# The layer norm's weights: from a multiply of the rows on GpSimd to a multiply of W1 on ScalarE

## The chip, the cores and the metric

The kernel runs on one core of one Trainium2 chip. The metric is the device time of the program in microseconds (us); the time before is the median of three runs. One further execution was taken by the hardware profiler: its trace is what the profile shows.

The engines are called as in the profile: PE is TensorE (PEld its weight loads), DVE is VectorE, ACT is ScalarE, POOL is GpSimd, SP is SyncE, from whose queue all DMAs of this kernel are issued. Each engine works through its own instructions in a fixed order and stops at one whose inputs are not there yet.

## The reference

Attention over 8 batches, 8 heads, 576 positions, head size 64, with a mask by blocks of 64 positions; then a layer norm and a two-layer perceptron with a residual.

```python
scores = scale * np.matmul(q, k.transpose(0, 1, 3, 2))
scores = np.where(block_i >= block_j, scores, -1000000000.0)
attn = np.exp(scores - max); attn = attn / (sum + 1e-09)
x = (attn @ v)  # heads side by side: 8 x 576 rows of 512

mu, var = mean(x), mean((x - mu) ** 2)
xn = (x - mu) / np.sqrt(var + 1e-06) * g_ln
ch = np.maximum(xn @ w_ch1, 0.0) @ w_ch2      # 512 -> 2048 -> 512
return x + ch
```

`g_ln` has 512 values, one for each column of `xn`, that is one for each row of `w_ch1`.

## The kernel before

All work is written as tasks, `add(engine or engines, cost, function, r=reads, w=writes, prio=...)`. A planner (`Plan.run`, L91) goes through them in a simulated time of its own, with cost estimates for each engine and for the DMAs, gives a task that may run on several engines to one of them, and so writes the order of every engine's instructions before the program is compiled. A task that is added, removed or given another engine shifts the planner's times, and with them the order of many others, also of tasks that the edit doesn't name.

**Attention.** 32 pairs of heads, one after the other on PE (`pair`, counted from 0 here). Each has scores (PE, L396), mask and row maximum (DVE, L411), exponentials with row sums (ACT, L414), transposes (PE, L423) with their evacuation into `pt` (ACT or DVE, by the helper lines L215 and L217) and the product with V (PE, L429 and L433), whose result is transposed by DVE (L506, `ot`) and stored to DRAM in `xd`. Four times two further steps treat the first block of 64 positions (L543 to L582). Beside all this the packed weights are unpacked (`decode`: ACT, DVE and POOL, L325 to L358) into `w1f` and, for W2, `wcs` in DRAM.

**Perceptron.** 36 tiles of 128 rows are treated in five rounds of 8, 8, 8, 6 and 6 tiles. For each round `norm_tiles` treats the tiles in pairs: load (`x<-xd`, L627, four or eight small DMAs for a tile), division by the softmax sums (L636, DVE or POOL), a copy for the residual (`xrow`, L640), statistics (L645), reciprocal square root (DVE L654 to L657, POOL L663 to L666), subtract and multiply (L671, DVE), the multiply by g (L674, POOL), a transpose (L676, DVE, `xnt`) and the way through DRAM (`xw`, L680; `xt`, L684) to the transposed tile `xt`. `operands` makes from these the left operands `xm` of a seven-product scheme (differences `tt` L701, high parts by L215 or L217, low parts L712). In round 0 these steps run beside the attention.

W1 and W2 are cut into 8 groups. In round 0 `stream` loads a group of W1 (`wf<-w1f`, L765; 128 partitions, 2 blocks, 512 columns in the order of W1's rows), forms sums on POOL (L773), high parts (L215 or L217) and low parts (L784, DVE or POOL) into `wa` and `wb`, and stores these to DRAM as `was` and `wbs`; in later rounds it loads them back (L758). The first three groups are made in the last pairs of the attention, the others during round 0. `products` multiplies a group with the operands (PE, L814, seven tasks of six matmuls; evacuations L822, L827, RELU L833 on ACT and low part L834 on DVE), and `second` multiplies the result `h` with W2 (PE, L874, `y`) and adds it to `ya` (DVE, L883). In the last group of a round the sums are stored (`out_t`, L886).

The high and low parts are two float32r numbers for each value, and each product is three matmuls. An `x` tile has two buffers, and so has `wf`.

The weights g lie in SBUF as `g_sb`, before as 512 values repeated in every partition (L297 to L300).

## Time and profile before

| | |
|---|---|
| median of 3 runs | 1068.18 us (1067.79 to 1070.01) |
| the profiled execution | 1069.32 us, span 1067.5 us |
| granted TensorE clock in it, mean | 0.996 |
| ACT multiplies by g | none |
| POOL multiplies by g (L674) | 36, 48.4 us busy |
| DMA | 248.91 MB, mean 233 GB/s |

In the lines of the profile "out<-in" stands for the tile or tensor that is written and those that are read. A group's line ends with its busy time, the mean duration of one in ns, the engine's idle time just before them, and what ended most of it. In the timeline a row is a run of like instructions with its start and its duration in us, and in brackets the idle time before it and its releaser.

### The profile page before, as it was taken

The numbers are of one execution on the slowest core, as the hardware profiler recorded it, in microseconds if no ns is written. First come the engines' busy times: TensorE is split into PE (matmuls) and PEld (weight loads), VectorE is DVE, ScalarE is ACT, GpSimd is POOL, SyncE is SP. The second block draws the span as 40 slices with busy tenths as digits, with TensorE's granted clock in tenths as the row PEclk, the third lists the DMA queues.
The fourth block names the chain that finished last, engine by engine and source line by source line (L and its number), as shares of the span: only waits on it lengthen the run. The fifth ranks groups of instructions, "written<-read, shape, count | busy, mean of one in ns | idle before, by whom it ended". The sixth has DMA issues, their size and how long they took to land.

```text
span 1067.5 us, 17862 instructions
## 1 busy us (share of the span) xinstructions
PE 1049.8 (98%) x6240; PEld 856.0 (80%) x6240; DVE 789.0 (74%) x1726; ACT 450.2 (42%) x1099; POOL 292.4 (27%) x442
## 2 busy tenths in 40 slices
PE   9999999999999999999999999999999999999998
PEld 6777767667678888778888888888888888889997
DVE  6878999998978889795666794676484766854554
ACT  7767979879874333242121151121132212322221
POOL 0002546534525766270212240221010221200000
PEclk9999999999999999999999999999999999999999
DMA  5447898998979888867777746777537779865541
GB/s 188 153 141 233 216 307 271 310 296 276 324 238 321 254 305 285 259 224 256 208 235 228 222 176 249 222 206 243 170 128 277 226 255 285 272 225 215 193 159 73
DMA packets 237930, 248.91 MB, mean 233 GB/s; under 512 B 159376, under 2 KB 188048, under 8 KB 227600
## 3 DMA queue, kind: packets, MB, share of 16 engines
q1 hardware_dynamic: 237840, 247.77, 71.5%
q8 instruction: 49, 0.80, 0.3%
q14 instruction: 41, 0.34, 0.1%
HBM read 182.71 MB, written 65.01 MB: 232 GB/s over the span
## 4 chain that ended last, share of the span: by engine, by line
PE 55%; DVE 5%; POOL 2%; DMA 2%; issue 1%; SPq 1%; ACT 0%; DVEq 0%; POOLq 0%
PE y L874 30%; PE p L814 25%; DVE h L834 1%; DVE ya L883 1%; SPq L627 1%; DMA wcs<-wd 1%; DMA wc<-wcs 1%; DVE t L827 0%; POOL x L674 0%; DVE xnt L676 0%; DVE xm L712 0%; DVE wb L784 0%; DVE wa L784 0%; DVE st L645 0%; DVE sgn L342 0%
## 5 line engine op out<-in xcount | busy, mean ns | idle before, releaser
L874 PE MATMUL y<-wc,h 128*128 128x512 f32 x1728 | 438.0, 392 | 2.1 <-ACT h L833 1.8
L874 PEld LDWEIGHTS y<-wc,h 128*128 128x128 f32 x1728 | 323.7, 188 | 66.4 <-DVE h L834 2.5
L883 DVE TENSOR_TENSOR ya<-y,ya 128x512 f32<-128x512 f32 x288 | 197.2, 686 | 155.1 <-PE y L874 154.4
L814 PE MATMUL p<-xm,wa 128*128 128x512 f32 (+1 forms) x960 | 222.5, 368 | 0.1
L814 PEld LDWEIGHTS p<-xm,wa 128*128 128x128 f32 x960 | 176.2, 188 | 27.3 <-DVE xm L712 0.6
L833 ACT ACTIVATE h<-t 128x512 fp32r<-128x512 f32 (+1 forms) x120 | 62.4, 581 | 275.9 <-DVE t L827 265.9
L814 PE MATMUL p<-xm,wb 128*128 128x512 f32 (+1 forms) x720 | 167.5, 368 | 1.7 <-DVE wb L784 1.5
L814 PEld LDWEIGHTS p<-xm,wb 128*128 128x128 f32 x720 | 132.5, 188 | 23.6 <-DVE wb L784 1.9
L822 ACT COPY t<-p 128x512 f32<-128x512 f32 (+1 forms) x120 | 65.3, 545 | 192.6 <-PE p L814 189.2
L827 DVE TENSOR_TENSOR t<-p,t 128x512 f32<-128x512 f32 (+1 forms) x120 | 75.8, 632 | 42.5 <-PE p L814 40.1
L396 PE MATMUL s<-raw 64*128 64x192 f32 (+4 forms) x640 | 96.5, 435 | 1.3 <-DVE nm L411 0.6
L414 ACT ACTIVATE pab<-pab,nm 128x576 f32<-128x576 f32 (+1 forms) x128 | 91.6, 724 | 8.9 <-DVE nm L411 8.7
L396 PEld LDWEIGHTS s<-raw 64*128 64x128 f32 x640 | 60.7, 186 | 37.8 <-issue 29.5
L411 DVE CUSTOM_DVE_ANT_0 pab<-s,never 128x576 f32<-128x576 f32 (+1 forms) x128 | 83.7, 683 | 3.4 <-PE s L396 3.0
L414 ACT ACTIVATE pu<-pu,nm 128x320 f32<-128x320 f32 (+1 forms) x128 | 64.5, 508 | 38.9 <-DVE nm L411 38.7
L433 PE MATMUL o<-pt,v 128*64 128x256 f32 (+1 forms) x768 | 80.3, 344 | 0.0
L333 POOL TENSOR_SCALAR mag<-mag 128x512 f32<-128x512 f32 x32 | 51.0, 1597 | 103.6 <-ACT mag L330 103.6
L433 PEld LDWEIGHTS o<-pt,v 128*64 128x64 f32 x768 | 56.9, 137 | 26.0
L834 DVE SCALAR_TENSOR_TENSOR h<-t,h 128x512 fp32r<-128x512 f32 (+1 forms) x120 | 76.9, 694 | 0.3 <-ACT h L833 0.2
L423 PE MATMUL tr<-ident,pab 128*128 128x128 f32 x512 | 67.1, 280 | 5.2 <-DVE nm L411 2.6
L215 ACT COPY pt<-tr 128x512 f32<-128x512 f32 (+1 forms) x126 | 65.0, 580 | 3.1 <-PE tr L423 2.7
L423 PEld LDWEIGHTS tr<-ident,pab 128*128 128x128 f32 x512 | 57.4, 143 | 11.0 <-DVE pt L217 3.7
(89 smaller groups left out, 982.8 us busy)
## 6 DMA issues: line engine op xcount, KB each, us to landing
wc<-wcs SPq DMA_DIRECT2D x40, 1024.0 KB, 6.8
wa<-was SPq DMA_DIRECT2D x32, 1024.0 KB, 7.6
wb<-wbs SPq DMA_DIRECT2D x32, 768.0 KB, 5.7
raw<-qk SPq DMA_DIRECT2D x32, 576.0 KB, 5.0
wr<-w SPq DMA_DIRECT2D x32, 512.0 KB, 6.7
v<-v SPq DMA_DIRECT2D x32, 320.0 KB, 5.2
x<-xd SPq DMA_DIRECT2D x144, 64.0 KB, 3.8
xrow<-x SPq DMA_DIRECT2D x36, 256.0 KB, 5.4
```

Of the source, the lines that this page charges most:

```text
L215: e.copy(out=out, in_=in_)
L396: nc.tensor.matmul(x, raw.t[HALF[h], 0, col], raw.t[HALF[h], 1, at:at + x.shape[1]], start=True, stop=True)
L411: add("DVE", dve(n) + .01, lambda: nc.vector.tensor_tensor_reduce(out=p.t[:, part(i, h)], in0=s.t[:, cols], in1=hide, scale=-0.125, scalar ...
L414: add("ACT", act(n, True) + .14, lambda: nc.scalar.activation(out=p.t[:, part(i, h)], in_=p.t[:, part(i, h)], func=AF.Exp, bias=nm.t[:, at ...
L423: nc.tensor.transpose(o.t[:, n * P:(n + 1) * P], x, ident)
L433: nc.tensor.matmul(o.t[HALF[h], at + lo:at + 256], v_sb.t[:, ck, HALF[h]], rhs(h), start=False, stop=(n == len(steps) - 1), skip_group_che ...
L814: nc.tensor.matmul(x.t[:, 0:TN], w_(l), xs[m].t[:, 0:half, o, k], start=start and k == e == 0, stop=k == 1 and e == 2, skip_group_check=True)
L822: add("ACT", act(TN), lambda: nc.scalar.copy(out=t.t[:, 0:TN], in_=x.t[:, 0:TN]), r=[r], w=[new], prio=0)
L827: add("DVE", dve(TN), lambda: nc.vector.tensor_add(t.t[:, 0:TN], x.t[:, 0:TN], t.t[:, 0:TN]), r=r, w=[new], prio=0)
L834: add("DVE", dve(TN), lambda: nc.vector.scalar_tensor_tensor(out=x.t[:, 1, 0:TN], in0=src(), scalar=0.0, in1=x.t[:, 0, 0:TN], op0=ALU.max, ...
L874: nc.tensor.matmul(yb.t, x.t[:, l, at:at + P], wc.t[:, i, o], start=i == e == 0, stop=i == 1 and e == 2)
L883: add("DVE", dve(512), lambda yb=yb, ya=ya: nc.vector.tensor_add(ya.t, yb.t, ya.t), r=[part, before_], w=[now], prio=1)
```

## The change

The load of g brings 4 values to each partition instead of 512: the host stores g as (4, 128) transposed, so that column c of `g_sb` holds the weights of rows 128c to 128c+127 of W1, one per partition. In `norm_tiles` the task of L674 is gone and the transposes read the rows as L671 leaves them. In `stream`, in round 0, one new task for each group runs four `nc.scalar.mul` in place on the loaded W1 group, each on two blocks of 128 columns (128x256 values) with one column of `g_sb` as the factor, and all that read the group now read the scaled one.

```diff
-    g_sb = odd.tile([P, DM], F32, name="g_sb")
+    g_sb = odd.tile([P, NC], F32, name="g_sb")
     gb = Buf()
-    gsrc = bass.AP(tensor=g.tensor, offset=g.offset, ap=[[0, P], [1, DM]])
-    add("SP", .45, lambda: nc.sync.dma_start(out=g_sb, in_=gsrc), w=[gb], prio=150, size=P * 2048)
+    add("SP", .45, lambda: nc.sync.dma_start(out=g_sb, in_=g), w=[gb], prio=150, size=P * 16)
...
-            unit, scaled = Buf(parent=x), Buf(parent=x)
+            unit = Buf(parent=x)
...
-            add(any_of(lambda e, x=x: e.tensor_mul(x.t, x.t, g_sb), POOL=pool(512)), r=[unit, gb], w=[scaled], prio=prio)
             xnt, xw = new_xnt(), new_xw()
-            add("DVE", dve(512), lambda x=x, xnt=xnt: nc.vector.transpose(xnt.t, x.t), r=[scaled], w=[xnt], prio=prio)
+            add("DVE", dve(512), lambda x=x, xnt=xnt: nc.vector.transpose(xnt.t, x.t), r=[unit], w=[xnt], prio=prio)
...
         fetch(2, 3)
+        raw = wf
+        wf = Buf(parent=raw)
+
+        def by_g():
+            for c in range(NC):
+                x = raw.t[:, :, P * c:P * c + P]
+                nc.scalar.mul(x, x, g_sb[:, c:c + 1])
+        add("ACT", 4 * act(256, True), by_g, r=[raw, gb], w=[wf], prio=prio)
...
-        "g": gl.reshape(1, -1).copy(),
+        "g": np.ascontiguousarray(gl.reshape(4, 128).T),
```

The planner's new order. Line numbers after the change are lower by one or two in the first part and higher by up to six behind the new task: the product is L814 before and L820 after, `y` L874 and L880, `ya` L883 and L889, the multiply by the sums L636 and L635, the mask L411 and L410.

On DVE, where the last masks of pair 13 stand, before (a row of `ISA` is a mask with its row maximum or the read of that maximum; `xm`, `st`, `norm` are those named above):

```order
L411 ISA pab,nm<-s,never 128x576
L411 ISA nm 128x1
L411 ISA pab,nm<-s,never 128x448
L411 ISA nm 128x1
L217 CAST xm_1623<-xt 128x256
L217 CAST xm_1626<-tt 128x256
L636 TENSOR_TENSOR x<-x,sums_all 128x512
L712 TENSOR_TENSOR xm_1626<-tt,xm_1626 128x256
L645 BN_STATS st<-x 128x6
L646 BN_AGGR norm<-st 128x2
```

and in the changed program:

```order
L410 ISA pab,nm<-s,never 128x576
L410 ISA nm 128x1
L635 TENSOR_TENSOR x<-x,sums_all 128x512 x2
L644 BN_STATS st<-x 128x6
L645 BN_AGGR norm<-st 128x2
L644 BN_STATS st<-x 128x6
L645 BN_AGGR norm<-st 128x2
L581 STREAM_TRANSPOSE ot_1639<-o 128x256 x2
L653 TENSOR_SCALAR norm<-norm 128x2
L655 TENSOR_SCALAR norm<-norm 128x2
L656 TENSOR_SCALAR norm<-norm 128x2
L410 ISA pab,nm<-s,never 128x448
```

Both tiles' multiplies, their statistics and the first step of the reciprocal root now stand ahead of the pair's last mask; before, they stood behind it, the second of them in the next pair.

On PE at the end of round 0, where the last group's products, its `y` and round 1's first products meet, before (the product with `xm_1540` is the first of a group's seven, the one that reads `xm_1704` the last):

```order
L874 MATMUL y<-wc,h 128x512 x24
L814 MATMUL p<-xm_1540,wa 128x512 x6
L814 MATMUL p<-xm_1559,wa 128x512 x6
L814 MATMUL p<-xm_1626,wa 128x512 x6
L874 MATMUL y<-wc,h 128x512 x18
L814 MATMUL p<-xm_1623,wa 128x512 x6
L814 MATMUL p<-xm_1688,wb 128x512 x6
L814 MATMUL p<-xm_1693,wb 128x512 x6
L874 MATMUL y<-wc,h 128x512 x6
L814 MATMUL p<-xm_1704,wb 128x512 x6
L874 MATMUL y<-wc,h 128x512 x6
L814 MATMUL p<-xm_1540,wa 128x512 x6
```

and in the changed program (here `xm_1523` marks the first of the seven and `xm_1744` the last):

```order
L820 MATMUL p<-xm_1710,wb 128x512 x6
L880 MATMUL y<-wc,h 128x512 x12
L820 MATMUL p<-xm_1525,wa 128x512 x6
L880 MATMUL y<-wc,h 128x512 x6
L820 MATMUL p<-xm_1744,wb 128x512 x6
L880 MATMUL y<-wc,h 128x512 x54
L820 MATMUL p<-xm_1523,wa 128x512 x6
L820 MATMUL p<-xm_1545,wa 128x512 x6
L820 MATMUL p<-xm_1708,wa 128x512 x6
L820 MATMUL p<-xm_1531,wb 128x512 x6
```

Before, the last `y` tasks of round 0 stand between the products of round 1; now nine of them (54 matmuls) run in one row and round 1's products follow in another.

On SP at the same place, before (`wf` is the last W1 group, `xw` and `xt` the pieces of round 1's tiles):

```order
L680 DMA xw<-xnt 32x16x32 x7
L758 DMA wc<-wcs 128x2048
L680 DMA xw<-xnt 32x16x32
L684 DMA xt<-xw 128x4x128
L627 DMA x<-xd 32x16x32 x8
L684 DMA xt<-xw 128x4x128
L792 DMA wbs<-wb 128x1536
L765 DMA wf<-w1f 128x1024
```

and in the changed program, from the load of the last W1 group on; rows between the two pieces are left out:

```order
L763 DMA wf<-w1f 128x1024
L682 DMA xt<-xw 128x4x128
L639 DMA xrow<-x 128x512
L756 DMA wc<-wcs 128x2048
L798 DMA wbs<-wb 128x1536
L678 DMA xw<-xnt 32x16x32 x8
```

```order
L678 DMA xw<-xnt 32x16x32
L682 DMA xt<-xw 128x4x128
L892 DMA out_t<-ya 128x512 x6
L682 DMA xt<-xw 128x4x128
L892 DMA out_t<-ya 128x512
```

The load of the last W1 group has moved ahead of pieces of round 1's tiles behind which it stood, and the second `xt` of round 1's last pair stands behind six stores of round 0's results. On DVE, in the changed program, the rows at the same place are these:

```order
L710 TENSOR_TENSOR xm_1744<-tt,xm_1744 128x256
L889 TENSOR_TENSOR ya<-y,ya 128x512 x8
L217 CAST xm_1523<-xt 128x256
L699 TENSOR_TENSOR tt<-xt 128x256
L710 TENSOR_TENSOR xm_1523<-xt,xm_1523 128x256
L217 CAST xm_1545<-tt 128x256
```

Eight additions to `ya` stand ahead of the last operand pieces of round 1's first product, which reads `xm_1523`.

## Prediction

> **What bounds the kernel now.** I read the page first, its busy rows and the chain that ended last, then stretches of time, then the matmuls' own timeline at the places where a stretch shows TensorE less than full.
>
> ```profile
> span 1067.5 us, 17862 instructions
> PE 1049.8 (98%) x6240; PEld 856.0 (80%) x6240; DVE 789.0 (74%) x1726; ACT 450.2 (42%) x1099; POOL 292.4 (27%) x442
> PE 55%; DVE 5%; POOL 2%; DMA 2%; issue 1%; SPq 1%; ACT 0%; DVEq 0%; POOLq 0%
> ...
> 162.74:171.53 8.79, 8.79 (x78) 6.53 (x77) 8.53 (x23) 7.65 (x22) 6.37 (x7) 1.00 0.88 227
> ...
> 171.53:181.72 10.19, 10.19 (x79) 7.09 (x77) 10.19 (x29) 10.10 (x28) 7.36 (x16) 1.00 1.00 371
> 181.72:192.23 10.51, 9.90 (x110) 7.07 (x109) 9.73 (x29) 9.78 (x29) 4.66 (x5) 1.00 0.74 180
> 192.23:201.78 9.55, 9.49 (x76) 6.64 (x77) 9.26 (x30) 8.45 (x24) 6.02 (x7) 1.00 1.01 292
> 201.78:213.33 11.55, 10.88 (x143) 8.02 (x141) 11.41 (x34) 9.74 (x29) 8.18 (x19) 1.00 1.00 347
> ...
> 250.00:270.00 20.00, 20.00 (x203) 14.64 (x199) 15.73 (x48) 20.00 (x56) 8.62 (x8) 1.00 0.80 274
> ...
> 440.00:460.00 20.00, 18.11 (x72) 14.19 (x71) 16.65 (x33) 5.66 (x11) 11.36 (x20) 0.91 0.81 297
> 460.00:480.00 20.00, 18.28 (x79) 14.49 (x79) 18.67 (x40) 9.22 (x24) 14.75 (x15) 1.00 0.71 233
> 480.00:1064.00 584.00, 583.75 (x2716) 499.96 (x2715) 373.09 (x681) 132.10 (x272) 88.78 (x180) 1.00 0.66 215
> ```
>
> A stretch's columns are its length, then busy time of PE, PEld, DVE, ACT and POOL, the clock, the DMA share and GB/s. Three things are to be seen. From 480 us on TensorE is busy 583.75 of 584.00 us: nothing that the other engines save there can shorten the run. In the attention, which ends near 317 us, DVE and ACT fill their stretches (10.19 and 10.10 of 10.19). And between 440 and 480 us TensorE lacks 1.89 and 1.72 us and has a lower clock in the first half. So the change can only be worth something in the attention and in the hand-over from round 0 to round 1. A busy TensorE in the attention isn't at its peak, since a matmul that waits may be drawn long; there I go by the time from one pair's scores to the next. The first five stretches run from the scores of one pair to those of the next: the undisturbed pair takes 8.79 us, the four behind it 10.19, 10.51, 9.55 and 11.55.
>
> **The change: removed and added work.**
>
> ```profile
> L674 POOL TENSOR_TENSOR x<-x,g_sb 128x512 f32<-128x512 f32 x36 | 48.4, 1355 | 21.9 <-DVE x L671 19.4 <-DMA wa<-was 1.4 <-DMA ya<-xrow 0.7
> L676 DVE STREAM_TRANSPOSE xnt<-x 128x512 f32<-128x512 f32 x36 | 25.3, 704 | 7.3 <-POOL x L674 7.2
> L215 ACT CAST xm<-tt 128x256 fp32r<-128x256 f32 x46 | 16.8, 408 | 10.3 <-POOL tt L701 5.1 <-PE p L814 3.8 <-POOL xm L712 1.4
> L414 ACT ACTIVATE pu<-pu,nm 128x320 f32<-128x320 f32 x64 | 36.0, 563 | 37.8 <-DVE nm L411 37.8
> L414 ACT ACTIVATE pu<-pu,nm 128x192 f32<-128x192 f32 x64 | 29.1, 454 | 1.0 <-DVE nm L411 0.9
> ```
>
> GpSimd loses 36 multiplies of 1355 ns, 48.4 us. It is 27% busy and has 2% of the chain, so this is worth only what its lateness costs: DVE stood 7.2 us before the transposes for it, about 0.2 us in each of 36. Each tile is ready 1.36 us sooner. The load of g shrinks to 2 KB per core; nobody waited for the old one.
>
> ScalarE gains 32 multiplies of 128x256 with one value per partition. The trace has none. Below it stands the cast of the same size without such a value, 408 ns; above it the exponential of 128x320 with a bias per partition, 563 ns; halfway in size between that and the 192-wide one (454) is 508. I take 0.46 us, halfway between 408 and 508: 1.84 us for a group's four, 14.7 us for the eight groups (13.1 to 18.0). [...] Five of the eight groups are made in round 0, where ACT is busy 43.86 of 112 us (the row stands further down), and TensorE's products are their cover; if that cover were gone they would cost 9.2 us. Three groups, 5.5 us, are made in the last pairs of the attention. There ACT is busy 20.00 of 20.00 us, so these are on the path unless DVE takes something over, which it does in part: DVE has 15.73 of 20.00, and the planner moves casts and evacuations of `pt`. The bounds are 0 and 5.5 us. Since TensorE is full beside ACT in that stretch, a pair takes whichever is longer, and I take +1.0, with the one product that no longer stands between the last two PV blocks in it.
>
> **Moved: pair 13's masks.** The new order runs both multiplies by the softmax sums (L636 of before) ahead of the last mask of this pair.
>
> ```profile
> 131.98 2.91 PE L396 MATMUL s<-raw 64*128 64x320 f32 x20
> ...
> 136.65 0.66 PE L423 MATMUL tr<-ident,pu 128*128 128x128 f32 x4 [1.17 <-DVE norm L654]
> 137.88 3.66 PE L423 MATMUL tr<-ident,pab 128*128 128x128 f32 x16 [0.57 <-DVE nm L411]
> ...
> 144.65 1.56 PE L396 MATMUL s<-raw 64*128 64x320 f32 x10
> ...
> 310.29 1.91 PE L423 MATMUL tr<-ident,pab 128*128 128x128 f32 x16
> ...
> 134.14 0.69 DVE L636 TENSOR_TENSOR x<-x,sums_all 128x512 f32<-128x512 f32 x1 [2.33 <-DMA x<-xd]
> ...
> 135.09 0.69 DVE L645 BATCH_NORM_STATS2 st<-x 128x6 f32<-128x512 f32 x1
> ...
> 130.67 0.76 DVE L582 STREAM_TRANSPOSE ot<-o 128x256 f32<-128x256 f32 x2
> ...
> 127.41 0.61 DVE L411 CUSTOM_DVE_ANT_0 pab<-s,never 128x448 f32<-128x448 f32 x1
> ...
> DMA to landing us min/median/max: 2.0/3.9/10.9
> ```
>
> The last row is the landing of the pieces of x (L627). Pairs are counted from 0; 131.98 is the start of pair 14. Before, DVE stood 2.33 us for the second tile until 134.14, behind that came the masks of pair 14, and the pair took 12.67 us (131.98 to 144.65) instead of 8.79: 3.9 us lost, of which 1.75 by sixteen transposes that ran in 3.66 us after the idle (1.91 in the last pair, at 310.29). In the changed program the same wait stands one pair sooner. Behind it in DVE's order come the second tile's multiply and statistics (0.69 and 0.69), two `ot` transposes (0.76), some 0.6 us of small steps and the mask that frees the score banks (0.61): 3.4 us from the landing to that mask's end. Before, this mask was done at 128.0, 4 us ahead of pair 14's scores, so there is that much room. If the eight pieces land at 131 to 132, since they follow each other on SP without gaps now, the scores start at 134.4 to 135.4 and a clean pair then brings pair 15 to 143.2 to 144.2 instead of 144.65; with the slow transposes again that is +0.3 to +1.3. Bounds: a landing at 129 or sooner gives 3.4 back, one at 135.5 loses 5.0 (rival 2). I take +0.5.
>
> **Moved: the third and fourth norm, 171.53 to 213.33.** These four stretches lose 10.19+10.51+9.55+11.55-4x8.79 = 6.6 us against clean pairs. Some 2 us of that is a first block's own work on TensorE, which stays: three steps of 32 small matmuls, 0.69 us each by the row below.
>
> ```profile
> 171.00:215.00 44.00, 0.69 (x32) 0.56 (x32) 1.00 0.94 300
> ```
>
> That leaves 4.6 us, and DVE is full or nearly so in all four (10.19 of 10.19 to 11.41 of 11.55), so an instruction taken off it there counts. The third norm's tiles come sooner by the 1.36 us of the missing multiply and the new order brings their transposes ahead into pairs where DVE had room; the pair with the softmax of a first block and the one behind it hand one multiply (0.69 us above), the reciprocal of the sums and five `pt` evacuations to their neighbours, which are full in part themselves. Bounds: 0, and -4.6. I take -1.0 for the first of these stretches (it lost 1.4) and -2.2 for the other three (3.2).
>
> **Moved: round 0 to round 1.**
>
> ```profile
> 447.25 0.63 ACT L215 CAST wa<-wf 128x512 fp32r<-128x512 f32 x1 [11.55 <-DMA wcs<-wd]
> ...
> L765 SPq DMA_DIRECT2D wf<-w1f x8: 326/430/659, 255.4 to 440.5; - x8
> ...
> 450.49 6.33 PE L874 MATMUL y<-wc,h 128*128 128x512 f32 x18 [1.81 <-ACT h L833]
> 456.66 4.24 PE L814 MATMUL p<-xm,wa 128*128 128x512 f32 x18
> ...
> 468.30 2.56 PE L814 MATMUL p<-xm,wb 128*128 128x512 f32 x10 [1.51 <-DVE wb L784]
> ...
> 472.43 1.66 PE L814 MATMUL p<-xm,wb 128*128 128x512 f32 x6 [0.21 <-DVE t L827]
> ```
>
> The last W1 group's load was issued at 440.5, behind tile pieces on SP's queue, and landed with ACT already waiting in front of its cast; the RELUs behind that cast came late. The price: 1.81, then 18 matmuls in 6.33 instead of 4.24 us (2.09, the clock 0.91), 1.51 and 0.21, in sum **5.6 us**. In the new order that load stands ahead of those pieces and the last group's products are interleaved as in other groups; I count these 5.6 as gone. What is late next: nine `y` tasks run in one row, and round 1's first product follows only after the `ya` additions of the last eight and the operand made from the second tile.
>
> ```profile
> L883 DVE TENSOR_TENSOR ya<-y,ya 128x512 f32<-128x512 f32 x288 | 197.2, 686 | 155.1 <-PE y L874 154.4
> L217 DVE CAST xm<-xt 128x256 fp32r<-128x256 f32 x16 | 4.8, 313 | 0.8 <-PE p L814 0.8
> L701 DVE TENSOR_TENSOR tt<-xt 128x256 f32<-128x256 f32 x16 | 7.4, 467 | 3.0 <-DMA xt<-xw 2.9
> L712 DVE TENSOR_TENSOR xm<-xt,xm 128x256 fp32r<-128x256 f32 x37 | 15.1, 448 | 0.0
> ...
> DMA to landing us min/median/max: 2.6/3.8/9.8
> ...
> 318.00:430.00 112.00, 111.82 (x493) 91.87 (x492) 98.65 (x163) 43.86 (x80) 68.77 (x85) 1.00 0.88 288
> ```
>
> After the last `y` come 0.69+0.31+0.47+0.45 = 1.9 us on DVE: the least that TensorE stands. The second tile's `xt` load (landing as in the row) follows on SP six `out_t` stores, each of which waits for a `ya`; the sixth result is two tasks (2x1.41 us) ahead of the last, its addition and the store's issue take 1.2, so the load goes out some 1.5 us ahead of the last `y`'s end, lands 3.8 later, and the stand is then 2.3+0.9 = 3.2. I take 2.7 us of standing, and, as at 450.49, 2.1 for the slow clock behind it: 4.8, so -0.8 net. With the landing of 9.8 the standing is 9.2 us and the net +5.7; with 1.9 and no slow clock it is -3.7. [...]
>
> **The sum**, against the profiled execution (1069.32 us, 1.1 above the median of the three runs; its span is 1067.5): +1.0 +0.5 -1.0 -2.2 -0.8 = -2.5, that is 1066.8 for that execution. The shift applied to the median 1068.18 gives **1065.7 us**.
>
> **The rivals.** (1) Nothing to measure: gains in attention are taken up elsewhere, since DVE and ACT are both full beside each other and an engine that comes early waits for the next, and one stall of 4.8 us stands in place of another of 5.6. For it speaks that the removed engine has 2% of the chain. With half of the gain in the four stretches the terms are -1.6-0.8+1.0+0.5 = -0.9, about 1067.3; with none of it 1068.9. (2) Slower, by the pieces of x ahead of pair 13's last mask. If the second tile lands at 135.5, 1.4 us later than before (the landings reach 10.9 us), that mask ends at 138.9 and pair 15 starts at 147.7 instead of 144.65: +3.1, and +1.75 by the slow transposes. With +4.9 here, the four stretches better by 1.6 and the rest as forecast, the time is 1068.18+4.9-1.6+1.0-0.8 = 1071.7. It decides at a landing near 132: what comes later is loss. Against it: the new order begins these loads in one row. (3) Slower, by ACT in the last pairs: all 5.5 us on the path, as the full stretch suggests, and a first multiply that waits for its `wf` load in front of `pt` evacuations. With the rest as forecast that is 1068.18+5.5+0.5-3.2-0.8 = 1070.2, and 1071.7 with 1.5 us of that wait. [...] It decides where ACT's surplus per pair passes what its waits for DVE gave before.
>
> **How the numbers follow.** My forecast 0.46; rival 1 0.27; rival 2 0.14; rival 3 0.13. A measurement here can tell about 0.2%, 2.1 us, from no change: faster is below 1066.0, slower above 1070.3. The forecast's own range, by the bounds of the four stretches (-4.6 to -1.6) and of the hand-over (-3.7 to +0.5), is 1061.4 to 1068.6, and since its middle lies close to that limit a quarter of it (0.11) is within 0.2%; of rival 1 a fifth (0.05) is faster, where more than half of that gain comes through; of rivals 2 and 3 a third (0.09) is within, with a smaller price. So faster 0.40, same 0.42, slower 0.18. The range runs from 1061.0 (the forecast's good end) to 1071.5 (between the times of rivals 2 and 3).
>
> **What would show it.** Right: no matmul idle of ACT or `wb` origin between 440 and 472, one stand of 2 to 3.5 us before round 1's first product released by DVE, then slow matmuls; the pairs from 171.53 to 213.33 shorter by some 3 us in sum; the four multiplies at 1.6 to 2.0 us; TensorE full from round 1 on. Wrong: a DVE wait for x over 4 us before pair 14's scores, ACT-released PE idle from 260 us on, a stand of over 5 us at round 1, or a later round with TensorE no longer full, for which I see no cause.

## The result, and the profile after

| | median | runs | span of the profiled execution |
|---|---|---|---|
| before | 1069.15 us | 6 (1067.79 to 1072.43) | 1067.5 us |
| changed | 1076.56 us | 6 (1074.84 to 1078.63) | 1074.2 us |

The ratio is 1.0065, with a 95% interval of 1.0052 to 1.0079: **slower** by about 7 us, where 2.5 us less had been forecast, and above the range of 1061.0 to 1071.5. All medians below are of undisturbed executions; one of e8's five took 2115.57 us and is left out.

The page of the changed kernel first: its busy rows and the chain that ended last.

```profile
PE 1050.3 (98%) x6240; PEld 858.4 (80%) x6240; DVE 781.3 (73%) x1718; ACT 465.8 (43%) x1142; POOL 240.1 (22%) x403
...
PE 71%; DVE 6%; ACT 1%; issue 1%; DMA 1%; SPq 0%; POOL 0%; DVEq 0%; POOLq 0%
```

The work moved as it was meant to: POOL has 52.3 us less, ACT 15.6 more, TensorE's busy time is the same within 0.5. Nothing here says where 6.7 us of span went. The stretches do (columns as before), and so does TensorE's timeline around pairs 14 and 15:

```profile
130.35:139.20 8.85, 5.32 (x38) 3.97 (x36) 7.04 (x27) 4.77 (x15) 6.12 (x15) 0.91 0.91 302
139.20:145.92 6.72, 6.71 (x40) 4.55 (x41) 3.97 (x9) 5.85 (x14) 1.49 (x1) 0.61 0.92 308
...
151.50:159.30 7.80, 6.17 (x40) 4.45 (x40) 3.40 (x8) 4.01 (x10) 2.72 (x2) 0.78 1.01 262
...
480.00:500.00 20.00, 16.54 (x65) 12.94 (x64) 9.75 (x21) 3.28 (x7) 0.85 (x1) 0.91 1.01 384
500.00:1070.00 570.00, 569.87 (x2657) 488.74 (x2656) 361.64 (x663) 130.22 (x269) 63.93 (x162) 1.00 0.65 211
```

```profile
130.35 3.25 PE L395 MATMUL s<-raw 64*128 64x320 f32 x20
...
139.21 1.97 PE L422 MATMUL tr<-ident,pab 128*128 128x128 f32 x8 [3.54 <-ACT pt L215]
...
144.15 1.84 PE L432 MATMUL o<-pt,v 128*64 128x256 f32 x16
145.92 2.91 PE L395 MATMUL s<-raw 64*128 64x320 f32 x20
...
151.51 0.66 PE L422 MATMUL tr<-ident,pab 128*128 128x128 f32 x4 [0.79 <-DVE pt L217]
152.95 0.66 PE L422 MATMUL tr<-ident,pab 128*128 128x128 f32 x4 [0.79 <-DVE pt L217]
154.44 0.91 PE L428 MATMUL o<-pt,v 128*64 128x256 f32 x4 [0.83 <-ACT pab L413]
...
159.30 2.91 PE L395 MATMUL s<-raw 64*128 64x320 f32 x20
```

Pair 14 runs from 130.35 to 145.92, 15.57 us (12.67 before), and pair 15 to 159.30, 13.38 us (9.30 before): together 7.0 us more. TensorE stands 3.54 us in the first, and what follows runs at a clock of 0.61; in the second it stands three times 0.8 us, and the clock is 0.78. The rounds behind 500 us are as full as before.

The hand-over from round 0 to round 1, on TensorE and on DVE:

```profile
476.65 10.75 PE L880 MATMUL y<-wc,h 128*128 128x512 f32 x46 [0.17 <-DVE h L840]
488.38 0.50 PE L820 MATMUL p<-xm,wa 128*128 128x512 f32 x1 [0.98 <-DVE xm L217]
491.36 5.74 PE L820 MATMUL p<-xm,wa 128*128 128x512 f32 x17 [2.48 <-DVE xm L710]
...
490.55 0.43 DVE L699 TENSOR_TENSOR tt<-xt 128x256 f32<-128x256 f32 x1 [2.21 <-DMA xt<-xw]
```

The weights of the last group come in time, and round 1's first product waits for the second `xt`, which stands behind the six stores: 3.46 us of standing, then 17 matmuls in 5.74 us.

### The profile page after: what moved, and what is told of

It reads as the page before. It is cut to its first block, busy times and chain, and to the rows that moved or that the text cites. A ratio compares the mean times of both kernels' runs of the same rounds, so it can differ in the third digit from the quotient of the medians.

```text
span 1074.2 us, 17799 instructions
## 1 busy us (share of the span) xinstructions
PE 1050.3 (98%) x6240; PEld 858.4 (80%) x6240; DVE 781.3 (73%) x1718; ACT 465.8 (43%) x1142; POOL 240.1 (22%) x403
## 4 chain that ended last, share of the span: by engine, by line
PE 71%; DVE 6%; ACT 1%; issue 1%; DMA 1%; SPq 0%; POOL 0%; DVEq 0%; POOLq 0%
PE y L880 34%; PE p L820 30%; PE tr L422 2%; PE s L395 2%; PE o L432 2%; DVE ya L889 1%; DVE xm L710 1%; PE o L428 1%; DVE pab L410 1%; DMA xt<-xw 0%; DVE h L840 0%; DVE pu L410 0%; DMA x<-xd 0%; ACT xm L215 0%; DVE t L833 0%
## 5 line engine op out<-in xcount | busy, mean ns | idle before, releaser
L880 PE MATMUL y<-wc,h 128*128 128x512 f32 x1728 | 435.3, 391 | 0.2 <-DVE h L840 0.2
L880 PEld LDWEIGHTS y<-wc,h 128*128 128x128 f32 x1728 | 322.7, 188 | 63.3 <-DVE h L840 1.9
L889 DVE TENSOR_TENSOR ya<-y,ya 128x512 f32<-128x512 f32 x288 | 196.9, 685 | 169.2 <-PE y L880 167.6
L820 PE MATMUL p<-xm,wa 128*128 128x512 f32 (+1 forms) x960 | 224.0, 370 | 3.6 <-DVE xm L710 2.5
L820 PEld LDWEIGHTS p<-xm,wa 128*128 128x128 f32 x960 | 177.3, 189 | 31.8 <-DVE xm L710 3.4
L820 PE MATMUL p<-xm,wb 128*128 128x512 f32 (+1 forms) x720 | 167.1, 367 | 0.0
L820 PEld LDWEIGHTS p<-xm,wb 128*128 128x128 f32 x720 | 132.6, 188 | 21.2
L395 PE MATMUL s<-raw 64*128 64x512 f32 (+4 forms) x640 | 97.2, 435 | 2.4 <-DVE nm L410 1.2
L410 DVE CUSTOM_DVE_ANT_0 pab<-s,never 128x576 f32<-128x576 f32 (+1 forms) x128 | 83.2, 683 | 4.0 <-PE s L395 3.6
## 6 DMA issues: line engine op xcount, KB each, us to landing
wb<-wbs SPq DMA_DIRECT2D x32, 768.0 KB, 5.9
```

The source lines that it names most:

```text
L395: nc.tensor.matmul(x, raw.t[HALF[h], 0, col], raw.t[HALF[h], 1, at:at + x.shape[1]], start=True, stop=True)
L410: add("DVE", dve(n) + .01, lambda: nc.vector.tensor_tensor_reduce(out=p.t[:, part(i, h)], in0=s.t[:, cols], in1=hide, scale=-0.125, scalar ...
L820: nc.tensor.matmul(x.t[:, 0:TN], w_(l), xs[m].t[:, 0:half, o, k], start=start and k == e == 0, stop=k == 1 and e == 2, skip_group_check=True)
L880: nc.tensor.matmul(yb.t, x.t[:, l, at:at + P], wc.t[:, i, o], start=i == e == 0, stop=i == 1 and e == 2)
L889: add("DVE", dve(512), lambda yb=yb, ya=ya: nc.vector.tensor_add(ya.t, yb.t, ya.t), r=[part, before_], w=[now], prio=1)
```

## The experiments

For each run the profiled execution is cut in two: from the start of pair 2's scores to the start of pair 31's (**attention**), and from there to the end (**rest**). What lies ahead of pair 2 varies by up to 1.6 us between executions. The table gives these, and the medians, beside the changed kernel's and that of before. A ratio is to executions of the kernel before that were taken beside the run, whose medians lay between 1069.7 and 1070.6 us. The profiled execution is a single one and not always near the median: that of e1 took 1072.19 us, and e10, whose attention has the same order and work, spent 281.8 us in it where e1 has 285.3. e11, e12, e15 and e16 were executed twice each. The runs follow below in four groups.

| | attention | rest | median us | ratio to before, 95% interval |
|---|---|---|---|---|
| before | 282.2 | 766.9 | 1069.15 | |
| changed | 289.9 | 766.0 | 1076.56 | 1.0052 to 1.0079 |
| e1: work of the change, order of before | 285.3 | 765.5 | 1068.27 | 0.998 to 1.0006 |
| e13: no multiply by g, order of before | 281.3 | 762.7 | 1065.99 | 0.9954 to 0.9984 |
| e14: ACT multiplies doubled, order of before | 288.7 | 768.7 | 1078.51 | 1.0069 to 1.01 |
| e2: work of before, order of the change | 300.5 | 776.4 | 1097.05 | 1.0237 to 1.0278 |
| e3: no multiply by g, order of the change | 289.0 | 768.0 | 1078.04 | 1.0055 to 1.0089 |
| e5: planner sees only the POOL task go | 292.1 | 778.8 | 1091.58 | 1.017 to 1.0208 |
| e6: planner sees only the ACT task come | 282.8 | 782.6 | 1085.48 | 1.0111 to 1.0148 |
| e11, e15: before, planner's constant 1.52, 1.48 | 286.4, 288.3 | 781.4, 781.8 | 1088.21, 1091.34 | 1.0132 to 1.0206, 1.0184 to 1.0225 |
| e12, e16: changed, the same constant | 289.9, 287.2 | 776.4, 768.8 | 1085.61, 1075.5 | 1.0108 to 1.0181, 1.0036 to 1.0076 |

### Work and order taken apart

The planner fixes the order before anything is emitted, so a task can keep its place and do something else. **e1** plans the kernel of before, empties the POOL task, and emits the multiplies in front of a group's first reader:

```diff
-            add(any_of(lambda e, x=x: e.tensor_mul(x.t, x.t, g_sb), POOL=pool(512)), ...
+            add(any_of(lambda e: None, POOL=pool(512)), ...
...
+        scaled_ = []
+        def by_g():
+            if not scaled_:
+                scaled_.append(1)
+                for c in range(NC):
+                    x = wf.t[:, :, P * c:P * c + P]
+                    nc.scalar.mul(x, x, g_sb[:, c:c + 1])
...
-            add("POOL", pool(256), lambda: getattr(nc.gpsimd, op)(...
+            add("POOL", pool(256), lambda: (by_g(), getattr(nc.gpsimd, op)(...
```

> The order of the kernel before on all engines, with the work of the change: the POOL multiplies by g are left out of it, and each W1 group's four ACT multiplies stand in front of the first instruction that reads the group. If the planner's new order is what costs (theory): pairs 14 and 15 start as before (about 132 and 145 us), the time lies at 1066 to 1071 us, with 0 to 2 us lost to ACT from 260 to 315 us. If the moved work itself costs (rival): about 1076 us.

**e2** plans the changed kernel, empties `by_g`, and lets POOL multiply in front of each transpose; **e3** is e2 without that multiply.

```diff
-        add("ACT", 4 * act(256, True), by_g, r=[raw, gb], w=[wf], prio=prio)
+        add("ACT", 4 * act(256, True), lambda: None, r=[raw, gb], w=[wf], prio=prio)
...
-    lambda x=x, xnt=xnt: nc.vector.transpose(xnt.t, x.t)
+    lambda x=x, xnt=xnt: (nc.gpsimd.tensor_mul(x.t, x.t, g_sb), nc.vector.transpose(xnt.t, x.t))
```

> The order of the changed kernel, with the work of before: POOL multiplies the rows by g in front of each transpose, ACT multiplies nothing. Theory (order): 1074 to 1078 us, pair 14 again takes about 15.5 us. Rival (work): 1067 to 1070 us.

> The order of the changed kernel with no multiply by g at all; g is left out of the result. Theory (order): 1073 to 1077 us; the difference to the changed kernel is what the 32 ACT multiplies cost, expected 0 to 2 us. Rival (work): 1066 to 1070 us.

**e13** is the kernel before with the POOL task emptied and nothing in its place, **e14** is e1 with a second multiply behind each:

```diff
-            add(any_of(lambda e, x=x: e.tensor_mul(x.t, x.t, g_sb), POOL=pool(512)), ...
+            add(any_of(lambda e: None, POOL=pool(512)), ...
```

```diff
                     nc.scalar.mul(x, x, g_sb[:, c:c + 1])
+                    nc.scalar.mul(x, x, 1.0)
```

> The kernel before, in its own order, with the 36 POOL multiplies by g left out; g is left out of the result. If GpSimd's work had been hidden (theory): within 2 us of before. If the multiplies had been on the path: 1062 to 1066 us, and the ACT multiplies of the first experiment cost what this gains.

> The first experiment (work of the change, order of before) with each ACT multiply followed by one more of the same size, by 1.0: 64 instead of 32. If the 13.6 us of ACT multiplies are hidden there (theory): 0 to 2 us over the first experiment's 1068.27. If they are on the path and had been paid by the missing POOL work: 4 to 12 us over it.

Measured: the new work in the old order takes 1068.27 us, with an interval that contains no change; the new order without any of the work takes 1078.04, as slow as the changed kernel. The 7 us are the order's. The multiplies cost it nothing (1076.56 with them, 1078.04 without), and e2 took 1097.05, far above either expectation. Its order has no place for POOL's multiplies: each stands between two steps of DVE, which waits 30.6 us for them in sum (32 times, 2.1 us at the longest), where it waited 7.2 in the kernel before.

```profile
DVE xnt L675 <- POOL x L675: 30.6, 32, 2.1
```

In the old order the work does have a price. Without POOL's multiplies it takes 1065.99 us (0.9954 to 0.9984 of before), 3.8 less than the executions beside it and at the upper end of the rival's range: they were not wholly hidden, as the theory had it. By the medians the ACT multiplies give 2.3 of these 3.8 us back, and doubled they take 10.2 more, within the 4 to 12 of e14's rival. Their own cost is plain in the changed kernel (duration of one in ns, minimum, median and maximum):

```profile
L772 ACT ACTIVATE wf<-wf,g_sb x32: 492/496/535, 269.7 to 434.7; 128x256 f32<-128x256 f32 x32
```

Where they cost is shown by pair 27 of e1, on ACT and on TensorE:

```profile
265.88 1.73 ACT L774 ACTIVATE wf<-wf,g_sb 128x256 f32<-128x256 f32 x4
267.63 0.62 ACT L215 CAST wa<-wf 128x512 fp32r<-128x512 f32 x1
268.16 1.55 ACT L215 COPY pt<-tr 128x512 f32<-128x512 f32 x3
...
268.79 1.14 PE L422 MATMUL tr<-ident,pab 128*128 128x128 f32 x8 [1.03 <-ACT pt L215]
```

and, in e14, on TensorE:

```profile
269.06 1.97 PE L422 MATMUL tr<-ident,pab 128*128 128x128 f32 x8 [2.85 <-ACT pt L215]
```

The first group's four multiplies stand ahead of the evacuations that TensorE waits for. Pair 27 takes 9.41 us before, 11.00 in e1 and 13.96 in e14: 1.6 us for 1.7 us of multiplies, and 3.0 more for the second set, whose longer stand (2.85 us) is again followed by slow matmuls, the same eight transposes in 1.97 us instead of 1.14.

### Which edit spoils the order, and whether any edit does

**e5** takes the ACT task out of the changed kernel's plan (the multiplies are emitted as in e1); **e6** puts the POOL task back into it, empty:

```diff
-        add("ACT", 4 * act(256, True), by_g, r=[raw, gb], w=[wf], prio=prio)
```

```diff
+            add("POOL", pool(512), lambda: None, r=[unit, gb], w=[scaled], prio=prio)
-            ... nc.vector.transpose(xnt.t, x.t), r=[unit], ...
+            ... nc.vector.transpose(xnt.t, x.t), r=[scaled], ...
```

> The change's work; the planner sees that the POOL task is gone, but no ACT task: the four multiplies stand in front of the first reader of each W1 group, as in the first experiment. If the missing POOL task alone makes the order that loses: 1074 to 1079 us, pairs 14 and 15 together 27 to 29 us (21.97 before, 28.95 in the changed kernel). If the ACT task makes it: 1067 to 1071 us.

> The change's work; the planner still sees the POOL task (empty) and sees the new ACT task. If the missing POOL task makes the order that loses: the attention runs as before up to about pair 26, and the time is 1066 to 1071 us. If the ACT task makes it: 1074 to 1079 us.

Each half is worse than both together, so neither expectation holds for the time. The cut in two tells them apart: with the POOL task in the plan (e6) the attention takes 282.8 us, near the 282.2 of before, without it (e5) 292.1, so it is the missing task that gives the attention its new order. The load of g, smaller in both, does not. The rest is another matter. In e5 it is 11.9 us longer, in e6 15.6, here nearly all in one place:

```profile
470.91 10.74 PE L881 MATMUL y<-wc,h 128*128 128x512 f32 x46 [0.52 <-DVE h L841]
496.93 0.80 PE L821 MATMUL p<-xm,wa 128*128 128x512 f32 x1 [15.28 <-DVE xm L217]
...
496.58 0.29 DVE L217 CAST xm<-xt 128x256 fp32r<-128x256 f32 x1 [14.20 <-DMA xt<-xw]
```

It is the hand-over again: SP has put the last tile pair's pieces behind the stores of round 0. That suggests that a new order is a new draw, whatever caused it. **e11** and **e15** test it on the kernel before, whose work stays as it is, **e12** and **e16** on the changed one:

```diff
-BW, LAG, TAIL = 3.0e5, .65, 1.5
+BW, LAG, TAIL = 3.0e5, .65, 1.52
```

(In e15 and e16 the constant is 1.48.)

> The kernel before with one constant of the planner's DMA estimate changed from 1.50 to 1.52; the work is the same, the order is another. If any other order loses against the one that was found for this kernel (theory): 1074 to 1095 us. If the order only loses when the POOL task is missing: within 4 us of before.

> The changed kernel with the same constant changed in the same way. Theory: another draw, anywhere from 1070 to 1095 us, no better on the average than the kernel before with that constant.

> The kernel before with the same constant of the planner at 1.48. Theory (any other order loses): 1075 to 1095 us. Rival (only the missing POOL task spoils the order): within 4 us of before.

> The changed kernel with that constant at 1.48. Theory: another draw, 1070 to 1095 us.

A change of a constant by 1.3% costs the kernel before 18 to 22 us, of which 14.5 and 14.9 lie behind the start of pair 31 (in e11 TensorE stands 12.61 and 4.36 us at the hand-over):

```profile
498.22 0.80 PE L814 MATMUL p<-xm,wa 128*128 128x512 f32 x1 [12.61 <-DVE xm L217]
```

Their attention is 4.2 and 6.1 us longer with the POOL task in place, so that task is one way to disturb it among others. The changed kernel's two further draws are 1085.61 and 1075.5. So every one of seven re-planned orders (the change's own, e5, e6 and these four) lost 6 to 22 us against the one order that the kernel before has. At 1.48 the changed kernel is the faster of the two by 15.8 us; at 1.52 the two can't be told apart (2.6 us, with intervals that overlap).

### Pairs 14 and 15

ACT of the changed kernel stands until 135.19 before a step of the weights' unpacking whose load is late, and the exponentials of pair 14 stand behind it:

```profile
135.19 0.67 ACT L329 ACTIVATE mag<-wr 128x512 f32<-128x512 f32 x1 [2.89 <-DMA wr<-w]
...
127.54 0.69 DVE L635 TENSOR_TENSOR x<-x,sums_all 128x512 f32<-128x512 f32 x1 [0.89 <-DMA x<-xd]
```

The wait for x that the forecast's second rival spoke of is only 0.89 us. **e4** moves this unpacking step and the next behind pair 14's four exponentials (on ACT the two rows below, on DVE one step behind one mask). **e7** moves also the two x multiplies and their statistics behind pair 13's last mask. **e8** further hands three evacuations of pair 14's `pt` from DVE to ACT. The first lines show what moved on ACT in e4, the second what moved on DVE besides in e7, the third what changed for ACT and DVE in e8 (numbers of tiles left out):

```diff
-ACTIVATE mag<-wr 128x512
-ACTIVATE sgn<-wr 128x512
 CAST xm<-tt 128x256
 ACTIVATE pu,sums_all<-pu,nm 128x320
 ACTIVATE pu,sums_all<-pu,nm 128x192
 ACTIVATE pu,sums_all<-pu,nm 128x320
 ACTIVATE pu,sums_all<-pu,nm 128x192
+ACTIVATE mag<-wr 128x512
+ACTIVATE sgn<-wr 128x512
```

```diff
-TENSOR_TENSOR x<-x,sums_all 128x512 x2
+STREAM_TRANSPOSE ot<-o 128x256 x2
+ISA pab,nm<-s,never 128x448
+TENSOR_TENSOR x<-x,sums_all 128x512
 BN_STATS st<-x 128x6
 BN_AGGR norm<-st 128x2
+TENSOR_TENSOR x<-x,sums_all 128x512
...
-STREAM_TRANSPOSE ot<-o 128x256 x2
...
-ISA pab,nm<-s,never 128x448
```

```diff
                 evac(lambda h=h, i=i: pt0.t[:, h, :, i - 3], ...
+                if k == 14:
+                    plan.tasks[-1].to_act = True
...
+        if getattr(k, "to_act", False) and k.eng == "DVE":
+            fn = k.ways["ACT"][1]
```

> The changed kernel with two ACT instructions of one weight chunk's unpacking (the absolute value and the scaled copy that wait for its load until 135.19 us) put behind the four exponentials of pair 14 instead of ahead of them, and one DVE step of the same chunk behind one mask; nothing else moves. If ACT's wait for that load is what stops pair 14 (theory): its 15.57 us become 10 to 12, and the time 1070 to 1074 us. If DVE's tile steps ahead of pair 13's last mask do it (the forecast's rival 2): pair 14 stays above 14 us and the time within 1 us of the changed kernel.

> The changed kernel with the multiplies by the softmax sums of one tile pair (and what depends on them) put behind pair 13's last mask, and the two ACT steps of one weight chunk behind the exponentials of pair 14 as in the fourth experiment. If DVE's tile steps ahead of that mask and ACT's wait for the chunk are together what stops pair 14: it takes 9.5 to 12 us instead of 15.57 (14.29 with the second alone), the time 1072 to 1076 us, and pair 15 still takes about 13. If neither is on the path: pair 14 stays above 13 us.

> As the run before it, and three evacuations of pair 14's pt that stand on DVE ahead of pair 15's last mask are done by ACT instead. If these copies, each of which waits for the transposes that wait for the copy before it, are what stops pair 15: it takes 9 to 11 us instead of about 13.4, and the time is 2 to 4 us below the run before it, at 1069 to 1073 us. If pair 15 is only late because pair 14 was: it improves already in the run before, and not here.

| | pair 14 | pair 15 | median us |
|---|---|---|---|
| before | 12.67 | 9.30 | 1069.15 |
| changed | 15.57 | 13.38 | 1076.56 |
| e4 | 14.29 | 13.11 | 1078.92 |
| e7 | 15.36 | 11.69 | 1079.23 |
| e8 | 15.32 | 9.89 | 1077.49 |
| e9 | 12.56 | 13.41 | 1077.26 |
| e3, for comparison | 12.57 | 13.87 | 1078.04 |

Pair 14's length is a weak witness. The seven profiled executions that keep the order of before up to there (before, e1, e10, e13, e14, e17, e18) took 11.40 to 14.75 us for it, and e3, in the changed kernel's order and with nothing moved, 12.57: there x lands late (DVE waits 2.25 us for it, until 129.71), the unpacking's load costs ACT only 0.45 us, and TensorE stands 1.09 us. Pair 15 is the steady one, 8.79 to 9.31 us in those seven and 13.38 to 13.87 in the changed kernel, e3 and e9. TensorE's row in e3:

```profile
138.94 1.14 PE L423 MATMUL tr<-ident,pab 128*128 128x128 f32 x8 [1.09 <-ACT pt L215]
```

The theories of e4 and e7 fell: with ACT's wait gone, pair 14 still takes 14.29 us, and with the tile steps moved too 15.36. In e4 x landed later, and DVE waited 2.01 us for it; in e7, with the mask ahead of it all, DVE has the two tiles' steps, the operand steps and a transpose between that mask and pair 14's first mask, from 129.32 to 135.14, without any wait:

```profile
128.80 0.58 DVE L439 CUSTOM_DVE_ANT_0 pab<-s,never 128x448 f32<-128x448 f32 x1
...
129.32 0.69 DVE L668 TENSOR_TENSOR x<-x,sums_all 128x512 f32<-128x512 f32 x1
...
135.14 0.47 DVE L439 CUSTOM_DVE_ANT_0 pu<-s,never 128x320 f32<-128x320 f32 x1
```

Such a block of 5.8 us, wherever it stands in this pair, is what these runs share; that it alone sets pair 14's length wasn't isolated. In pair 15 the three copies cost 1.8 us (11.69 to 9.89, one execution each). The 1.69 us between 13.38 and 11.69 is the clock: the 32 matmuls behind the same three gaps take 4.86 us in the changed kernel and 3.17 in e7. But none of this came out at the end. e8's attention is 288.1 us against 289.9 in the changed kernel; pair 15's gain is given back in the pairs behind it, and the single executions of e7 alone spread from 1075.27 to 1081.66.

**e9** repeats one group of four transposes seven times over, in the place where TensorE stood 3.54 us:

```diff
-    pe(k + 1, 3, 4 * .112, turn(o, slots), ...
+    again = (lambda t=turn_: [t() for _ in range(8)]) if k == 13 and (h, i) == (0, 3) else turn_
+    pe(k + 1, 3, 4 * .112, again, ...
```

> The changed kernel; one group of four transposes in the slot of pair 14 is done eight times instead of once (the same values into the same bank), about 3 us of work for TensorE in the place where it stands 3.54 us. If the slow matmuls behind that stand come from the stand itself: the clock from 139 to 146 us is 0.9 or more instead of 0.61, the 16 PV steps take 3.2 us instead of 4.8, pair 14 takes 12.5 to 14 us instead of 15.57, and the time falls by 1.5 to 3 us. If the clock falls for another reason (traffic, the load of the other engines): it stays at about 0.6 and the time stays or rises.

```profile
140.50:143.68 3.18, 3.18 (x33) 2.14 (x32) 3.18 (x8) 3.07 (x8) 1.11 (x1) 1.00 0.98 303
152.25:157.09 4.84, 4.84 (x32) 3.28 (x32) 1.91 (x6) 1.89 (x4) 2.73 (x2) 0.65 1.06 286
```

```profile
141.11:145.92 4.81, 4.81 (x33) 2.98 (x33) 2.06 (x6) 3.94 (x10) 1.49 (x1) 0.65 0.94 312
154.44:159.30 4.86, 4.86 (x32) 3.58 (x32) 1.92 (x6) 1.89 (x4) 2.72 (x2) 0.65 1.07 269
```

The first fence has e9's PV steps of pairs 14 and 15 as stretches, the second those of the changed kernel. Without a gap they run at full clock, 3.18 us instead of 4.81, and pair 14 takes 12.56; pair 15, whose gaps were not filled, keeps its 0.65. That the filler did it isn't shown: ACT's copies came sooner in that execution (137.67 against 138.60), so that by an estimate from these rows TensorE would have stood some 1.7 us, not 3.54, and e3, without a filler, has the same pair 14, and its eight transposes behind 1.09 us of standing take 1.14 us, where the changed kernel's take 1.97. The time did not fall either (1077.26): the attention is 2.0 us shorter than in the changed kernel's profiled execution, 1.1 than in e3's, and the rest 2.5 longer than the former's.

What the slow clock hangs on, all the traces together tell better. The changed kernel first, then e7:

```profile
134.22:137.64 3.42, 1.45 (x12) 1.02 (x10) 1.86 (x6) 2.45 (x8) 3.29 (x5) 1.00 1.00 363
137.64:144.46 6.82, 5.25 (x26) 3.71 (x28) 5.34 (x14) 6.82 (x20) 1.80 (x2) 0.50 0.79 255
...
151.29:154.70 3.41, 1.57 (x11) 1.08 (x13) 1.91 (x4) 2.33 (x8) 0.00 (x0) 1.00 0.94 254
154.70:158.12 3.42, 3.42 (x21) 2.53 (x19) 1.66 (x6) 1.89 (x4) 2.09 (x2) 0.50 1.13 285
```

```profile
149.01:152.43 3.42, 2.64 (x24) 2.20 (x21) 2.94 (x11) 3.42 (x12) 0.00 (x0) 1.00 0.84 210
152.43:155.84 3.41, 1.79 (x16) 1.22 (x16) 2.24 (x5) 2.11 (x7) 0.00 (x0) 1.00 0.99 285
...
155.09:158.26 3.17, 3.17 (x32) 2.48 (x32) 1.91 (x6) 1.92 (x4) 1.52 (x2) 1.00 1.19 288
```

In these traces the granted clock is either full or half, and changes only at points that are whole multiples of 3.41 us apart (137.64, 144.46, 154.70 and 158.12 here); where they lie differs between executions (137.80, 141.22, 451.83 and 455.24 in the kernel before). Cut into such steps, with the first 25 and the last 20 us left out, the twenty traces have 31 steps at full clock in which TensorE stood 1.95 us or more in sum: half clock followed each of them. It followed none of the 57 with 0.90 to 1.48 us, and 19 of the 45 in between. So as far as these traces go it is the standing summed over a step that counts. The three gaps of pair 15 put 1.84 us into one step in the changed kernel; in e7 they fall into two, with 0.78 and 1.62 us, and the clock stays full.

### Towards a faster version

Three runs start from e1. **e10** moves one load and one store on SP:

```diff
-DMA xw<-xnt 32x16x32 x7
 DMA wc<-wcs 128x2048
-DMA xw<-xnt 32x16x32
+DMA wbs<-wb 128x1536
+DMA wf<-w1f 128x1024
+DMA xw<-xnt 32x16x32 x8
 DMA xt<-xw 128x4x128
 DMA x<-xd 32x16x32 x8
 DMA xt<-xw 128x4x128
-DMA wbs<-wb 128x1536
-DMA wf<-w1f 128x1024
```

> The first experiment (work of the change, order of before) with one edit on SP: the load of the last W1 group and one store of wb stand ahead of the eight pieces of one tile pair and the ten DMAs behind them, instead of behind. If that load's place is what costs at the end of round 0: the stands of ACT (9.4 us) and TensorE (1.4, 1.6 and 1.2 us) there go, and the time is 1062 to 1066 us, below both kernels. If it is the group's data that come late (its unpacking): no change, 1068 us.

The load now lands before ACT needs it, and the stand for `wb` is gone. The one ahead of it is not:

```profile
449.60 1.67 ACT L858 ACTIVATE h<-t 128x512 fp32r<-128x512 f32 x3 [12.49 <-DVE t L852]
...
450.80 6.36 PE L899 MATMUL y<-wc,h 128*128 128x512 f32 x18 [1.83 <-ACT h L858]
...
439.97 0.69 DVE L649 TENSOR_TENSOR x<-x,sums_all 128x512 f32<-128x512 f32 x1 [3.65 <-DMA x<-xd]
442.02 0.69 DVE L649 TENSOR_TENSOR x<-x,sums_all 128x512 f32<-128x512 f32 x1 [1.36 <-DMA x<-xd]
```

ACT waits for DVE, and DVE had waited 5.0 us for x in front of the work that the RELUs need. The kernel before has the same two waits on DVE, which end at 439.29 and 441.77 (2.12 and 1.79 us); in e10 they are 1.1 us longer in sum, behind two more DMAs on SP. A run with x sooner was not made. The median is 1070.74, 0.9999 to 1.0029 of before: no gain.

**e17** moves the first group's multiplies and cast behind pair 27's exponentials on ACT, **e18** also this group's three steps on DVE:

```diff
-ACTIVATE wf<-wf,g_sb 128x2x128 x4
-CAST wa<-wf 128x2x256
...
+ACTIVATE wf<-wf,g_sb 128x2x128 x4
+CAST wa<-wf 128x2x256
```

```diff
-TENSOR_TENSOR wa<-wf,wa 128x2x256
-CAST wa<-sum 128x2x256
-CAST wb<-sum 128x2x256
...
+TENSOR_TENSOR wa<-wf,wa 128x2x256
+CAST wa<-sum 128x2x256
+CAST wb<-sum 128x2x256
```

> The first experiment (work of the change, order of before) with the first W1 group's four ACT multiplies and the cast behind them put behind the four wide exponentials of pair 27, instead of ahead of the three evacuations of pt; one POOL sum moves by one place with them. If these multiplies in front of the evacuations are what ACT's work costs: pair 27 takes 9.4 us as before instead of 11.0, and the time is 1065 to 1067 us, under both kernels. If ACT lacks the time wherever they stand: pair 27 or 28 stays 1.6 us longer and the time at 1068 us.

> As the run before it (first W1 group's multiplies on ACT behind the wide exponentials of pair 27), with DVE's three steps for this group (one low part, two casts) put behind the wide masks of pair 28 instead of between the steps of pair 27. If the wait for these was all that the run before lost: pair 27 takes 9.4 us and pair 28 11 to 12, and the time is 1065 to 1068 us. If the three steps disturb pair 28 where they stand now: 1068 to 1072 us.

In both, pair 27 has its 9.41 and 9.42 us back, so the place was right. In e17 DVE then stood for that group, and TensorE for DVE:

```profile
276.37 5.54 PE L408 MATMUL s<-raw 64*128 64x320 f32 x18 [5.83 <-DVE sums_all L529]
...
271.97 0.72 DVE L807 TENSOR_TENSOR wa<-wf,wa 128x512 fp32r<-128x512 f32 x1 [3.75 <-ACT wa L228]
```

Pair 28 took 19.07 us, in e18 13.81 (11.41 in e1); the medians are 1075.76 (1.0028 to 1.0061) and 1071.88 (1.0014 to 1.0038). No version that computes the reference was found to beat the kernel before.

## Why the prediction was wrong, step by step

**Removed POOL work, "worth only what its lateness costs".** Mis-sized. In the old order it is worth 3.8 us by the medians (e13). Its profiled execution, one of the faster ones, is 4.2 us shorter behind pair 31's start: the stand of 1.81 us at the hand-over and the slow matmuls behind it are gone there.

**Added ACT work.** The price of four multiplies was taken at 1.84 us and is 1.70 (1.69 to 1.73 in the eight groups): one takes 496 ns in the median, more than the 0.46 us assumed, but the four of a group overlap. The term of +1.0 us for the last pairs is 1.6 in pair 27 of the old order. In the changed kernel pairs 27 to 30 take 1.2 us more than before, which looks like the forecast, but e3, without the multiplies, takes 1.5 more there: the size was right by luck. No run gave the multiplies to DVE; in the order of before, e13 puts the most that such a move can bring at the 2.3 us between it and e1.

**Pair 13's masks, +0.5 us.** This is the step that failed first, and the next one is as large. It priced one wait (x at 131 to 132 us) and put "a clean pair" behind it. x landed at 127.5, sooner even than the good bound of 129, and pair 14 started 1.6 us earlier than before; then pairs 14 and 15 took 7.0 us more, so that pair 16 starts 5.4 us later (159.30 against 153.95) where +0.5 had been forecast. The forecast compared DVE's order at the mask alone, while ACT's unpacking, DVE's block of tile steps and the copies of `pt` had moved in the two pairs behind it as well. The second rival (slower, by x) named the place and the sign, but not the mechanism: in the changed kernel's trace x was early and a weights' load late, and e3, where x was the late one, has the same long pair 15. Which of the moved steps sets these two pairs was not isolated, but for the copies of `pt` in pair 15.

**Third and fourth norm, -1.0 and -2.2 us.** This step failed as well. Pairs 18 to 21 take 42.25 us after and 41.80 before; they gained nothing, and pair 17, ahead of them, takes 9.93 instead of 8.79. From pair 16 to pair 22 that is +1.6 us where -3.2 had been forecast. Shorter sums of DVE work in a pair were counted as time, without asking what ACT and SP would do there; which of them took the gain was not looked into. With the 5.4 us ahead of it this is 6.9 us at the start of pair 22, and the rest of the run adds nothing: +0.7 up to pair 31 and -0.9 behind it.

**Round 0 to round 1, -0.8 us.** Right by its stated steps: 3.46 us of standing and 17 matmuls in 5.74 where 4.0 is full speed (18 in 4.24 at 456.66 in the kernel before), in sum 5.2 us, against 4.8 forecast and 5.6 before. The reading of the old loss was not right: in the kernel before DVE, after its waits for x, reaches the step that needs the late weights only as they arrive (447.9 us), and e10, with the weights early, keeps a first stand of 1.83 us and is rid only of the 1.51 for `wb`.

**The clock.** The forecast set 2.1 us of slow matmuls behind its stand, after the row at 450.49, and 1.7 came. Stands of 2.48 us here and of three times 0.8 us in pair 15 were followed by clocks of 0.91 and 0.78 over their stretches, and in pair 14 the half clock begins at 137.64, when TensorE had stood 1.97 of the 3.54 us. The length of one stand does not decide: in the kernel before 1.51 us at 468.30 was followed by full clock, while each gap of pair 15 is only some 0.8 us. What counts in these traces is their sum in a step of 3.41 us.

**What was left out.** No term or rival stood for the replanning itself. The sum took the new order as about as good as the old one outside the places that were looked at. By e11 and e15 it should have started from the opposite: each of the seven other orders that were timed loses 6 to 22 us. That the kernel's constants were chosen with its one order in view would explain it; no run here shows how they were found.

## What to carry to other kernels

Where a planner writes the order, time an edit twice: once with the order held fixed and the work exchanged, once replanned. Only the first tells what the work is worth, and draws of the planner with a constant slightly changed tell what a new order costs. Repairing one wait of a statically ordered kernel can move the loss to another engine instead of removing it: e4, e7, e8, e10, e17 and e18 each repaired one, and none lowered the time. And a pair's length in one profiled execution is a weak witness: with the order unchanged, pair 14 took 11.40 to 14.75 us.

## What the runs showed of the hardware that was not expected

Several short stands of TensorE went before a halved clock: gaps of 0.79, 0.79 and 0.83 us within 3.7 us left the next 4.86 us at 0.65 (3.17 us for the same 32 matmuls in e7), and the same gaps did nothing in e7, where they fell into two steps of 3.41 us. A step with 1.95 us of standing or more was followed by half clock in all 31 cases, one with 0.90 to 1.48 us in none of 57. Work added on ACT in pair 27 did not cost in proportion: 1.7 us in front of the evacuations cost 1.6 us, and the next 1.7 us (four of 0.42) cost 3.0, with a clock of 0.97 from 250 to 318 us, where e1 has 1.00, and the eight transposes at 1.97 us instead of 1.14.
